# Linear attention and a gated feed-forward layer on one core: how the two weight matrices are brought in, with the column sums of w_out on TensorE and its centring on GpSimd

## The chip, the cores and the metric

The kernel runs on one core of a Trainium2 chip, as one launch. The core has five instruction queues that run beside each other: TensorE (PE in the profile, with its weight loads PEld), VectorE (DVE), ScalarE (ACT), GpSimd (POOL) and SyncE (SP, here only a queue that issues DMAs). The metric is the device time of one execution in microseconds (us), as the median of several runs; less is better. Three runs of the kernel before gave 724.57, 724.15 and 721.62 us, median 724.15 us.

## The reference

q, k and v are 8 x 8 heads of 576 x 64. Each goes through a feature map with 256 features, then linear attention; the 4608 x 512 result is the input of a feed-forward layer with a softmax gate and a layer norm.

```python
def phi(x):
    proj = np.einsum('bhsd,df->bhsf', x, w_phi)
    proj = proj - np.max(np.abs(proj), axis=-1, keepdims=True)
    return np.concatenate([np.exp(proj), np.exp(-proj)], axis=-1)
q_p, k_p = (phi(q), phi(k))
kv = np.einsum('bhsf,bhsd->bhfd', k_p, v)
z = np.sum(k_p, axis=2)
num = np.einsum('bhsf,bhfd->bhsd', q_p, kv)
den = np.einsum('bhsf,bhf->bhs', q_p, z)[..., None] + 1e-06
...                                   # x = num / den, as 4608 x 512
h = x @ w_in                          # 512 x 1024
e = np.exp(h - np.max(h, axis=-1, keepdims=True))
solu = h * e / (np.sum(e, axis=-1, keepdims=True) + 1e-09)
ln = (solu - solu.mean(-1)) / np.sqrt(solu.var(-1) + 1e-06) * g_ln
out = ln @ w_out                      # 1024 x 512
```

(The last three lines are shortened.) The weights w_in and w_out arrive as 64-bit floats.

## The kernel before, in words

The attention is done in 16 units (8 batches, 2 groups of four heads), and each unit in tiles of 128 positions. Per unit TensorE projects k and q (`pjk`, `pjq`), VectorE takes the largest absolute value (`m`) and subtracts it (`dk`, `dq`), TensorE transposes the q part (`dT`), ScalarE takes the exponentials (`ek`, `fq`), TensorE sums keys with values (`kvT`), and multiplies with the q features (`num`, `den`); GpSimd divides (`xa`, `xb`). From the fourth unit on q is projected in another form (`hq`, `pq`, `blk`, `pT`).

The feed-forward part takes 36 tiles of 128 tokens. Each needs 24 matmuls of 128x512 into `h` (high and low halves of x and of w_in: `mxh`, `mxl`, `win_h`, `win_l`) and 24 into `o` (`uhs`, `uls` with `w_out_h`, `w_out_l`). Its first tile can start only when the first batch is divided and all of `win_h` and `win_l` are there, and its first `o` when all of `w_out_h` and `w_out_l` are.

Bringing the weights in is the part that the change touches. There are eight tiles of 1 MB each, 0 to 3 of w_in and 4 to 7 of w_out. Each tile goes through these steps, whose names stand in the list of operations (line 457 on):

- `wl` (`w_load`, line 364): a DMA of the 64-bit words into `wraw`, on SP's queue.
- `ws` (`w_rebias`): ScalarE rescales the upper words, 128x1024.
- `wb` 0, 1 and 2 (`w_bits`, line 386): VectorE puts a 32-bit float `w` together from the two words, with one TENSOR_SCALAR and two SCALAR_TENSOR_TENSOR of 128x1024.
- for w_in: `wh` (ScalarE, `win_h`) and `wlo` (GpSimd, `win_l`).
- for w_out: `wg` (`w_gain`): ScalarE multiplies the rows with the layer norm's gain, 2 x 128x512. Then the mean over all 1024 rows is taken off, which stands for the layer norm's own mean: `wa` (`w_sum`) adds the four tiles on GpSimd, `cm` (`w_mean`) sums that over the partitions with two matmuls against a matrix of 1/1024, `cms` copies the result out of PSUM, `wc` (`w_center`) subtracts it on VectorE, eight times 128x512, and `woh` (ScalarE) and `wol` (GpSimd) make the high and low halves.

The order is written out: `SEQUENCE` (line 50) is a list of operation numbers, and each engine's queue holds its operations in the order in which they stand there. An engine never goes past an operation that waits. The planner's costs in the list of operations set nothing at this stage; buffers are given out in the order of `SEQUENCE` too, first in, first out for each tag. The raw tiles of w_in lie in the buffers `xa` and `xb`, where the divided attention output goes later, so tiles 0 to 3 pass through two buffers; those of w_out lie in the place of the finished `w_out_h` and `w_out_l`. Line 264 is the helper that records every instruction, so nearly all rows of the profile show that line and are told apart by their tiles.

Of the kernel before, what the change touches and what calls it, by code (L numbers as in the profile page):

```python
# [210 lines left out]
def dma(nbytes, spread=False):  # L211
    return (580 if spread else 440), max(nbytes / 300.0, 50)
# [63 lines left out]
def linear_attention_then_moe(ctx: ExitStack, tc, qT, qT2, kT, v, w_phi, w_in, g_ln, w_out, out):  # L276
# [134 lines left out]
    def w_sum(i):  # L411
        a = W[4].bitcast(F32) if i == 5 else W["sum"]
        if i == 5:
            W["sum"] = sb("e", [P, DF], F32, "wsum")
# [855 lines left out]
```

## Time and profile before

| | |
|---|---|
| median of three runs | 724.15 us |
| the profiled execution | 722.87 us |
| its span, first to last instruction | 721.1 us |
| busy: PE, PEld, DVE, ACT, POOL | 698.2, 519.0, 486.8, 369.7, 514.4 us |
| mean granted TensorE clock | 0.993 of full |
| DMA | 109.96 MB, mean 152 GB/s |

The profiled execution is 1.77 us longer than its span and 1.28 us under the median. Times in the trace count from the start of the span. A busy PE is not a PE at its peak, since matmuls are pipelined and their records overlap: the spacing of starts is the better price of one. An idle time is put down to the last event that released it.

### The profile page before, as it was taken

What the parts mean: (1) busy time and instruction counts of PE and PEld (TensorE: products, weight loads), DVE (VectorE), ACT (ScalarE), POOL (GpSimd) and SP (SyncE); (2) the same over time, 40 slices, a digit from 0 to 9 for tenths busy, and PEclk for the clock granted to TensorE, in tenths of its full rate; (3) what the DMA queues carried; (4) which work ended last, traced back from release to release, by engine and by line L of the source; (5) the groups of instructions that cost most, each with busy time, mean ns of one, the idle gap of its engine ahead of it and who ended that gap; (6) DMA issues with size and microseconds to landing.
All of it is one profiled execution on the core that took longest, in us unless ns stands there. A gap on an engine that the chain in (4) does not pass through costs nothing.

```text
span 721.1 us, 13381 instructions
## 1 busy us (share of the span) xinstructions
PE 698.2 (97%) x4858; PEld 519.0 (72%) x4858; DVE 486.8 (68%) x795; ACT 369.7 (51%) x683; POOL 514.4 (71%) x501
## 2 busy tenths in 40 slices
PE   5989799999999999999999999999999999999997
PEld 4655577777777777777767777777777777788886
DVE  5999977855777766677576668657666765446341
ACT  3878556544554564655555546436455355424131
POOL 1127799997799868888798988987777967344332
PEclk9999999999999999999999999999999999999999
DMA  7781257743654746564656365454665532521431
GB/s 265 271 263 63 68 166 207 200 141 105 192 174 126 195 148 208 141 184 135 168 160 196 122 180 163 124 155 132 180 163 141 175 107 80 170 67 53 132 128 55
DMA packets 113649, 109.96 MB, mean 152 GB/s; under 512 B 57648, under 2 KB 90928, under 8 KB 113072
## 3 DMA queue, kind: packets, MB, share of 16 engines
q1 hardware_dynamic: 113584, 109.11, 50.8%
q8 instruction: 39, 0.64, 0.4%
q14 instruction: 26, 0.21, 0.1%
HBM read 76.68 MB, written 32.39 MB: 151 GB/s over the span
## 4 chain that ended last, share of the span: by engine, by line
PE 78%; POOL 5%; DVE 2%; ACT 1%; DMA 1%; issue 1%; SPq 0%; POOLq 0%; ACTq 0%
PE o L264 25%; PE h L264 24%; PE kvT L264 9%; PE num L264 7%; PE pjk L264 4%; PE den L264 3%; PE pq L264 3%; POOL zt L264 1%; POOL hq L264 1%; POOL w_out_l L264 1%; DMA uTs<-du 1%; POOL uls L264 1%; POOL zacc L264 1%; POOL blk L264 1%; DMA rawq<-in_q 1%
## 5 line engine op out<-in xcount | busy, mean ns | idle before, releaser
L264 ACT ACTIVATE ek<-dk 128x512 f32<-128x512 f32 (+1 forms) x160 | 88.0, 583 | 65.6 <-DVE dk L264 65.1
L264 POOL TENSOR_TENSOR uls<-uTs,uhs 128x1024 fp32r<-128x1024 f32 x33 | 79.1, 2397 | 42.7 <-ACT uhs L264 34.6
L264 PE MATMUL o<-w_out_h,uhs 128*128 128x512 f32 x264 | 106.8, 405 | 0.0
L264 PE MATMUL o<-w_out_h,uls 128*128 128x512 f32 x264 | 104.2, 395 | 0.0
L264 PE MATMUL o<-w_out_l,uhs 128*128 128x512 f32 x264 | 104.1, 394 | 0.0
L264 PE MATMUL h<-win_h,mxh 128*128 128x512 f32 x288 | 93.4, 405 | 0.0
L264 PE MATMUL h<-win_l,mxh 128*128 128x512 f32 x288 | 89.6, 392 | 0.0
L264 PE MATMUL h<-win_h,mxl 128*128 128x512 f32 x288 | 89.4, 391 | 0.0
L264 POOL TENSOR_TENSOR zt<-ek 128x512 f32<-128x512 f32 x52 | 67.4, 1295 | 20.8 <-ACT ek L264 19.0
L264 DVE TENSOR_REDUCE nm<-h 128x1 f32<-128x1024 f32 x36 | 43.8, 1216 | 56.9 <-PE h L264 56.8
L264 POOL TENSOR_TENSOR hq<-rawq,hq 64x1152 fp32r<-64x1152 f32 x26 | 68.9, 2650 | 7.3 <-issue 3.4
L264 PE MATMUL num<-fq,kvf 128*64 128x288 f32 x512 | 68.9, 412 | 1.6 <-DVE eu L264 0.9
L264 ACT ACTIVATE fq<-pT 128x576 f32<-128x576 f32 x104 | 67.6, 676 | 4.8 <-DVE pT L264 4.8
L264 DVE TENSOR_REDUCE m<-pjk 128x4 f32<-128x512 f32 (+1 forms) x80 | 48.8, 623 | 31.6 <-PE pjk L264 31.4
L264 ACT ACTIVATE eu<-h,nm 128x1024 f32<-128x1024 f32 x36 | 40.2, 1118 | 55.5 <-DVE nm L264 49.7
L264 DVE STREAM_TRANSPOSE blk<-pq 128x288 f32<-128x288 f32 x104 | 45.5, 459 | 30.4 <-PE pq L264 28.1
L264 PE MATMUL kvT<-ek,rawv 128*64 128x256 f32 x512 | 63.0, 389 | 0.0
L264 PEld LDWEIGHTS h<-win_h,mxl 128*128 128x128 f32 x288 | 54.0, 188 | 12.3
L264 PEld LDWEIGHTS h<-win_l,mxh 128*128 128x128 f32 x288 | 54.0, 188 | 12.2
L264 PEld LDWEIGHTS h<-win_h,mxh 128*128 128x128 f32 x288 | 50.8, 188 | 10.5 <-issue 1.1
L264 POOL TENSOR_TENSOR blk<-blk,mcol 128x1152 f32<-128x1152 f32 x26 | 55.4, 2132 | 3.8 <-ACT mcol L264 3.0
L264 PEld LDWEIGHTS o<-w_out_h,uls 128*128 128x128 f32 x264 | 49.7, 188 | 11.7
(107 smaller groups left out, 1425.3 us busy)
## 6 DMA issues: line engine op xcount, KB each, us to landing
du<-ub SPq DMA_DIRECT2D x33, 512.0 KB, 2.8
uTs<-du SPq DMA_DIRECT2D x132, 128.0 KB, 3.1
rawq<-in_q SPq DMA_DIRECT2D x26, 576.0 KB, 5.3
rb<-d SPq DMA_DIRECT2D x64, 144.0 KB, 3.5
out<-os SPq DMA_DIRECT2D x36, 256.0 KB, 3.1
rawk<-in_k SPq DMA_DIRECT2D x32, 256.0 KB, 3.8
rawv<-in_v SPq DMA_DIRECT2D x32, 256.0 KB, 4.0
dk<-kvs SPq DMA_DIRECT2D x28, 192.0 KB, 2.0
```

The costliest lines, as they stand in the source:

```text
L264: return self.tc.keep_in_program_order(method(*args, **kwargs))
```

## The change

Four things are changed.

- All eight weight loads (`wl`) are issued from ScalarE's queue instead of SP's.
- The three GpSimd additions `wa` and the tile `wsum` are gone. `cm` now reads the four tiles themselves: eight matmuls of 128x512 instead of two, accumulating into the same bank.
- The eight subtractions `wc` run on GpSimd instead of VectorE.
- `SEQUENCE` is written anew for the shorter list of operations, so all five queues are in a somewhat different order. The operations that are not named above are the same in number and form.

```diff
 SEQUENCE = (
-    99, 88, 0, 3, 2, 126, 89, 230, 4, 102, 7, 90, 132, 103, 136, 104, 105, 127, 107, 95, 198, 91, 100, 96, 101,
...
     def w_load(i, tag):
         if i < 4:
             raw = sb(tag, [P, DF, 2], U32, f"wraw{i}")
             src = w_in[i * P : (i + 1) * P, :].bitcast(U32).rearrange("p (f two) -> p f two", two=2)
-            nc.sync.dma_start(out=raw, in_=src)
+            nc.scalar.dma_start(out=raw, in_=src)
...
-            nc.sync.dma_start(out=raw4, in_=src)
+            nc.scalar.dma_start(out=raw4, in_=src)
...
-    def w_sum(i):
-        a = W[4].bitcast(F32) if i == 5 else W["sum"]
-        if i == 5:
-            W["sum"] = sb("e", [P, DF], F32, "wsum")
-        nc.gpsimd.tensor_tensor(out=W["sum"], in0=a, in1=W[i].bitcast(F32), op=ALU.add)
-
     def w_mean():
-        cm = bank("mo", [P, DM], "cmean")
-        for c in range(2):
-            nc.tensor.matmul(
-                cm, lhsT=ones_mean, rhs=W["sum"][:, c * DM : (c + 1) * DM], start=(c == 0), stop=(c == 1)
-            )
-        W["cm"] = cm
+        cm = W["cm"] = bank("mo", [P, DM], "cmean")
+        for i in range(4, 8):
+            for c in range(2):
+                w = W[i].bitcast(F32)[:, c * DM : (c + 1) * DM]
+                nc.tensor.matmul(cm, lhsT=ones_mean, rhs=w, start=i + c == 4, stop=i + c == 8)
...
     def w_center(f):
         w = W[4 + f // 2].bitcast(F32)[:, (f % 2) * DM : (f % 2 + 1) * DM]
-        nc.vector.tensor_tensor(out=w, in0=w, in1=W["cms"], op=ALU.subtract)
+        nc.gpsimd.tensor_tensor(out=w, in0=w, in1=W["cms"], op=ALU.subtract)
...
-        op(("wl", i), "sync", dma(8 * P * DF), z - 9, w_load, (i, raw_tag[i] if i < 4 else None), alloc=[(raw_tag[i], R)] if i < 4 else [])
+        op(("wl", i), "scalar", 200, z - 9, w_load, (i, raw_tag[i] if i < 4 else None), alloc=[(raw_tag[i], R)] if i < 4 else [])
...
-    op("cm", "tensor", 2 * 855, w_mean_at, w_mean, (), [("wa", 7)], [("mo", "cm")], ["wsum"])
+    op("cm", "tensor", 8 * 430, w_mean_at, w_mean, (), [("wg", i) for i in range(4, 8)], [("mo", "cm")],
+       [("w32", i) for i in range(4, 8)])
...
-        op(("wc", f), "vector", 602, z, w_center, (f,), ["cms"], tiles=["cms", T])
+        op(("wc", f), "gpsimd", 1290, z, w_center, (f,), ["cms"], tiles=["cms", T])
```

How the new order stands is seen at three places. In the names, `wraw_107`, `wraw_109`, `wraw_113`, `wraw_115`, `wraw_146` are the raw tiles 7, 1, 0, 4 and 6 of the changed kernel.

The first is the start of ScalarE's queue. Before, the queue begins with the conversion of w_phi and with the first exponentials, and its first `ws` (tile 0) is its sixth instruction:

```order
L264 ACT_TABLE_LOAD
L264 CAST w_hh<-wph 64x128 x2
L264 ACTIVATE ek<-dk 128x2x128
L264 ACTIVATE ek<-dk 128x4x128
L264 ACTIVATE wraw_116<-wraw_116 128x1024
L264 ACTIVATE ek<-dk 128x4x128 x2
```

With the change it begins with four loads of 1 MB, and two `ws` (tiles 1 and 7) follow each other ahead of three of the first unit's exponentials:

```order
L263 DMA wraw_107<-in_w_out 128x2x1024
L263 DMA wraw_109<-in_w_in 128x2048
L263 DMA wraw_113<-in_w_in 128x2048
L263 DMA wraw_115<-in_w_out 128x2x1024
L263 ACT_TABLE_LOAD
L263 ACTIVATE ek<-dk 128x2x128 x2
L263 DMA wraw_146<-in_w_out 128x2x1024
L263 ACTIVATE ek<-dk 128x4x128
L263 ACTIVATE wraw_109<-wraw_109 128x1024
L263 ACTIVATE wraw_107<-wraw_107 128x1024
L263 ACTIVATE ek<-dk 128x4x128 x2
```

So the loads are ahead of everything else of ScalarE, and SP's queue, from which they are gone, begins with w_phi and the first k, q and v.

The second is GpSimd's queue from its first division (`xa`) to the first `mxl`, on which the first matmul of the feed-forward part waits. Before (`wsum` is the sum of the w_out tiles, `w32_4` to `w32_7` are these tiles):

```order
L264 TENSOR_TENSOR xa_639<-E_350,rb_537 128x576
L264 TENSOR_TENSOR wsum_673<-w32_4_356,w32_5_477 128x1024
L264 TENSOR_TENSOR wsum_673<-wsum_673,w32_6_643 128x1024
L264 TENSOR_TENSOR wsum_673<-wsum_673,w32_7_671 128x1024
L264 TENSOR_TENSOR hq_770<-rawq_591,hq_770 64x1152
L264 TENSOR_TENSOR win_l_99<-w32_3_563,win_h_98 128x1024
L264 TENSOR_TENSOR w_out_l_908<-w32_5_477,w_out_h_903 128x512
...
L264 TENSOR_TENSOR mxl_1138<-xa_639,mxh_1105 128x512
```

With the change (`cms_815` is the mean):

```order
L263 TENSOR_TENSOR xa_620<-E_358,rb_505 128x576
L263 TENSOR_TENSOR win_l_99<-w32_1_223,win_h_98 128x1024
L263 TENSOR_TENSOR win_l_99<-w32_3_559,win_h_98 128x1024
L263 TENSOR_TENSOR hq_659<-rawq_541,hq_659 64x1152
L263 TENSOR_TENSOR w32_4_499<-w32_4_499,cms_815 128x512
L263 TENSOR_TENSOR w32_7_281<-w32_7_281,cms_815 128x512 x2
L263 TENSOR_TENSOR xa_620<-E_653,rb_804 128x576
L263 TENSOR_TENSOR w32_5_488<-w32_5_488,cms_815 128x512
L263 TENSOR_TENSOR w_out_l_923<-w32_7_281,w_out_h_872 128x512
L263 TENSOR_TENSOR w32_6_465<-w32_6_465,cms_815 128x512 x2
...
L263 TENSOR_TENSOR mxl_1163<-xa_620,mxh_1112 128x512
```

From the mean on, the queue now holds eight subtractions, the last `win_l`, three divisions and two `w_out_l` ahead of the first `mxl`; two of the `win_l` have moved ahead of the mean. After the first `mxl` six `w_out_l` are left, against five before.

The third is TensorE around the mean. Before, `cmean` stands behind the projection `pjk` of the third unit:

```order
L264 MATMUL kvT<-ek,ones_half 32x128 x4
L264 MATMUL pjk<-wph,rawk 128x256
L264 MATMUL cmean<-wsum,ones_mean 128x512 x2
L264 MATMUL dT<-ident,dq 128x128 x6
L264 MATMUL kvt<-ident,kvs 128x128 x3
```

With the change that projection is behind it:

```order
L263 MATMUL kvT<-ek,ones_half 32x128 x4
L263 MATMUL dT<-ident,dq 128x128 x3
L263 MATMUL cmean<-w_4_499,ones_mean 128x512 x2
L263 MATMUL cmean<-w_5_488,ones_mean 128x512 x2
L263 MATMUL cmean<-w_6_465,ones_mean 128x512 x2
L263 MATMUL cmean<-w_7_281,ones_mean 128x512 x2
L263 MATMUL pjk<-wph,rawk 128x256
```

Behind the mean TensorE does the same operations as before up to the first `h`, with one `pq` pair and one group of three `dT` more, which stood behind the first `h`.

More of the change, by code (lines that the diff above doesn't have):

```diff
@@ L467, in linear_attention_then_moe @@
             op(("wg", i), "scalar", 1260, z, w_gain, (i,), [("wb", i, 2), "gain"], tiles=[T])
-    for i in range(5, 8):
-        op(("wa", i), "gpsimd", 2330, w_mean_at - 2, w_sum, (i,),
-           [("wg", 4), ("wg", 5)] if i == 5 else [("wg", i), ("wa", i - 1)], [("e", "wsum")] if i == 5 else (),
-           [("w32", 4), ("w32", 5), "wsum"] if i == 5 else [("w32", i), "wsum"])
-    op("cm", "tensor", 2 * 855, w_mean_at, w_mean, (), [("wa", 7)], [("mo", "cm")], ["wsum"])
+    op("cm", "tensor", 8 * 430, w_mean_at, w_mean, (), [("wg", i) for i in range(4, 8)], [("mo", "cm")],
+       [("w32", i) for i in range(4, 8)])
     op("cms", "scalar", 478, w_mean_at, w_mean_out, (), ["cm"], [("m2k", "cms")], ["cm"])
```

272 rows, old and new, of the table SEQUENCE are left out of this document.

## The prediction

> **What bounds the kernel now.** I read the stages first (busy time of each engine in stretches of the span; the number behind an engine is its busy time in that stretch, the last three are the granted clock, the DMA share and GB/s).
>
> ```profile
> 0.00:18.00 18.00, 10.48 (x85) 8.54 (x87) 10.45 (x19) 6.93 (x14) 2.27 (x17) 0.91 0.79 265
> ...
> 36.00:54.00 18.00, 14.87 (x186) 9.62 (x182) 18.00 (x20) 13.83 (x28) 5.14 (x2) 1.00 0.83 263
> 54.00:72.00 18.00, 16.91 (x187) 10.46 (x188) 17.05 (x26) 15.71 (x33) 13.84 (x7) 0.91 0.20 63
> 72.00:90.00 18.00, 14.04 (x148) 9.22 (x149) 16.64 (x23) 9.97 (x23) 13.13 (x7) 0.91 0.28 68
> 90.00:108.00 18.00, 17.54 (x99) 13.46 (x99) 14.31 (x24) 9.87 (x22) 17.32 (x14) 1.00 0.59 165
> 180.00:252.00 72.00, 72.00 (x517) 53.17 (x516) 54.02 (x95) 37.57 (x69) 62.39 (x54) 1.00 0.58 171
> ```
>
> And from the page, TensorE's busy tenths in 40 slices of 18 us:
>
> ```profile
> PE   5989799999999999999999999999999999999997
> ```
>
> The columns of the stages are PE, PEld, DVE, ACT, POOL. There are two regimes. From 36 to 90 us VectorE is full or nearly so (18.00, 17.05, 16.64 of 18) and TensorE has holes. From 90 us on TensorE is full, 72.00 of 72 in the row from 180, and the page has 9 in every slice up to the last. All the changed work lies in the first regime, so the time changes by as much as TensorE comes earlier, or later, to the first matmul of the feed-forward part; what follows is the same TensorE work. That matmul, and the mean's, stand here in TensorE's timeline (start, duration, and in brackets the idle time before and its releaser):
>
> ```profile
> 55.09 0.55 PE L264 MATMUL dT<-ident,dq 128*128 128x128 f32 x3 [2.27 <-ACT dn L264]
> 55.56 2.89 PE L264 MATMUL kvT<-ek,rawv 128*64 128x256 f32 x16
> 60.73 0.70 PE L264 MATMUL pjk<-wph,rawk 128*128 128x256 f32 x2
> 61.27 1.88 PE L264 MATMUL cmean<-wsum,ones_mean 128*128 128x512 f32 x4
> 62.98 0.82 PE L264 MATMUL dT<-ident,dq 128*128 128x128 f32 x6
> 65.15 1.95 PE L264 MATMUL kvT<-ek,rawv 128*64 128x256 f32 x16
> 79.00 0.55 PE L264 MATMUL dT<-ident,dq 128*128 128x128 f32 x3 [3.71 <-DVE blk L264]
> 79.47 2.91 PE L264 MATMUL kvT<-ek,rawv 128*64 128x256 f32 x16
> 86.03 2.16 PE L264 MATMUL num<-fq,kvf 128*64 128x288 f32 x16 [0.25 <-DVE blk L264]
> 89.53 0.38 PE L264 MATMUL pq<-hq,w_hh 128*128 128x288 f32 x1
> 89.88 0.63 PE L264 MATMUL h<-win_h,mxh 128*128 128x512 f32 x2
> ```
>
> The same 16 `kvT` take 1.95 us at 65.15, but 2.89 and 2.91 us behind the holes at 55.09 and 79.00, in the two stretches whose granted clock is 0.91. So a hole costs its own length, and then its neighbours run slower: 0.95 us on these 16, and with the shorter records that end the group I take 1.7 us behind each hole, an estimate.
>
> **What slows VectorE.** The view of the tile `wraw` (shortest, median, longest ns), the subtractions' row of the costliest groups to 95 us (busy us, mean ns), and the worst rows of its timeline:
>
> ```profile
> L264 DVE SCALAR_TENSOR_TENSOR w<-wraw,w x16: 1209/1218/2945, 15.6 to 73.4; 128x1024 uint32<-128x1024 uint32 x16
> L264 DVE TENSOR_SCALAR w<-wraw x8: 642/688/2865, 14.2 to 67.2; 128x1024 uint32<-128x1024 uint32 x8
> L264 DVE TENSOR_TENSOR w<-w,cms 128x512 f32<-128x512 f32 x8 | 6.8, 892 | 0.1
> 30.46 2.94 DVE L264 SCALAR_TENSOR_TENSOR w<-wraw,w 128x1024 uint32<-128x1024 uint32 x1
> 47.60 1.84 DVE L264 SCALAR_TENSOR_TENSOR w<-wraw,w 128x1024 uint32<-128x1024 uint32 x1
> 49.37 2.87 DVE L264 TENSOR_SCALAR w<-wraw 128x1024 uint32<-128x1024 uint32 x1
> 67.24 2.14 DVE L264 TENSOR_SCALAR w<-wraw 128x1024 uint32<-128x1024 uint32 x1
> 70.62 2.37 DVE L264 SCALAR_TENSOR_TENSOR w<-wraw,w 128x1024 uint32<-128x1024 uint32 x1
> 73.41 2.88 DVE L264 SCALAR_TENSOR_TENSOR w<-wraw,w 128x1024 uint32<-128x1024 uint32 x1
> ```
>
> Each long one lies beside a GpSimd instruction:
>
> ```profile
> 29.93 2.39 POOL L264 TENSOR_TENSOR win_l<-w,win_h 128x1024 fp32r<-128x1024 f32 x1 [26.89 <-ACT win_h L264]
> 48.33 3.36 POOL L264 TENSOR_TENSOR wsum<-w,w 128x1024 f32<-128x1024 f32 x1
> 54.87 5.56 POOL L264 TENSOR_TENSOR wsum<-wsum,w 128x1024 f32<-128x1024 f32 x2 [3.19 <-ACT w L264]
> 71.88 3.34 POOL L264 TENSOR_TENSOR win_l<-w,win_h 128x1024 fp32r<-128x1024 f32 x1
> 78.67 1.27 POOL L264 TENSOR_TENSOR w_out_l<-w,w_out_h 128x512 fp32r<-128x512 f32 x1 [1.24 <-ACT w_out_h L264]
> 81.06 2.35 POOL L264 TENSOR_TENSOR win_l<-w,win_h 128x1024 fp32r<-128x1024 f32 x1 [1.13 <-ACT win_h L264]
> 83.37 1.42 POOL L264 TENSOR_TENSOR xa<-E,rb 128x576 f32<-128x576 f32 x1
> 87.75 1.29 POOL L264 TENSOR_TENSOR mxl<-xa,mxh 128x512 fp32r<-128x512 f32 x1 [0.73 <-ACT mxh L264]
> ```
>
> Ahead of the mean (seven tiles) the excess over the medians is 1.72 + 0.62 + 2.18 = 4.5 us; in tile 2, behind the mean, 1.45 + 1.15 + 1.66 = 4.3 us.
>
> **The parts, with their costs.** All times are on the trace of 722.87 us.
>
> *Loads on ScalarE's queue.* Issuing costs ScalarE about 0.45 us a load:
>
> ```profile
> L264 SPq DMA_DIRECT2D wraw<-in_w_in x4: 340/431/576, 4.4 to 47.6; - x4
> 11.58 1.13 ACT L264 ACTIVATE wraw<-wraw 128x1024 f32<-128x1024 f32 x1 [0.80 <-DMA wraw<-in_w_in]
> 14.00:16.00 2.00, 2.00 (x26) 1.95 (x24) 1.93 (x4) 0.58 (x2) 0.00 (x0) 0.64 0.98 365
> ```
>
> Four of the eight go out while ScalarE still waits for w_phi, so the issuing itself is hidden. But 4.2 MB now compete with the first k, q and v, and the transfers run at 365 GB/s where they are full. The first two `ws` want 2.1 MB: at half of 365 GB/s that is 11.5 us, from about 2 us on, so 13.5 us, against 11.58 before. VectorE reaches its first weight step at 14.2 us (first row of `TENSOR_SCALAR` above), with the `ws` of 1.13 us in between. Bounds: 0, and 10 us if the loads are served ahead of all else (4.2 MB / 365 GB/s = 11.5 us, less what SP can issue). I take 1.0 us late, since half each is nearest to what two full queues would do.
>
> The Trainium skill, *DMA: Bandwidth & Descriptors*, section "Issuing engines are not separate DMA queues", says that another issuing engine adds no DMA engine and saves issue time alone, and its section on queues that the engines take turns between the queues. By turns the start is late by the 1.0 us taken; no run here has two queues.
>
> *The three additions gone, eight matmuls for two.* Two matmuls of the mean start at 61.27, and the next begins at 62.98: 1.71 us, 0.855 each. Eight take 6.84 us, 5.13 us more TensorE work, in a stage where TensorE has holes. The mean needs no GpSimd any more, so it starts when TensorE gets there and the last gain (`wg`) is done:
>
> ```profile
> 55.80 1.33 ACT L264 ACTIVATE w<-w,gcol 128x512 f32<-128x512 f32 x2 [0.47 <-DVE w L264]
> 63.18 0.59 ACT L264 COPY cms<-cmean 128x512 f32<-128x512 f32 x1 [0.20 <-PE cmean L264]
> ```
>
> The gain ends at 57.13; 4.5 earlier and 1.0 later, at 53.6. TensorE: 61.27, less `pjk` that now stands behind (0.54), less 4.5, plus 1.0, is 57.2 with the slow clock from 55.56 on and 55.5 without it. I take 56.0. The mean then ends at 62.8, against 62.98: up to here the change wins nothing.
>
> *From the mean to the first `h`.* Before, that took 89.88 - 62.98 = 26.9 us, of which 3.96 are holes that wait for VectorE (3.71 + 0.25) and 1.7 slow clock. VectorE loses the eight subtractions from this stretch (6.8 us by eight times their mean of 0.89) and can be ahead by that much, so I take these 5.7 us as gone; I add `pjk` (0.54) and the `pq` pair and `dT` that moved ahead (0.35 and 0.47 by the starts of the rows behind them, 0.8 together). That is 22.6 us, so the first `h` starts at 85.4. Since 0.8 us of work that stood behind it now lies before it, TensorE is 89.88 + 0.8 - 85.4 = 5.3 us ahead.
>
> *Centring on GpSimd.* From the mean to the first `mxl` its queue holds eight subtractions at 1.27 (the `w_out_l` row, the same two-input form), three divisions at 1.42, one `win_l` at 2.35, two `w_out_l` at 1.27, and the `mxl` of 1.29: 10.2 + 4.3 + 2.35 + 2.5 + 1.3 = 20.6 us. From `cms` at 63.4 that ends at 84.0: hidden by 1.4 us, if nothing blocks it. ScalarE holds its `woh` in order behind each subtraction, with the exponentials for TensorE behind them. I take 1.0 us for such new waits, between 0 and the 4.3 us of tile 2's excess.
>
> **Sum:** +1.0 (start), -4.5 (bits), +5.13 (mean) and the rest as above: 5.3 - 1.0 = 4.3 us less, 718.6 us against the profiled 722.87. On the median, 1.28 us above that execution, 719.9 us.
>
> **Rivals.**
>
> *GpSimd takes VectorE's place (0.24).* If the subtractions and the bits of tile 2 block each other as at 71.88 and 73.41, the first `mxl` comes at 84.0 + 4.3 = 88.3, `h` at 88.6, and the gain is 2.0 us; one more `w_out_l` (1.27) is left for the stretch from 90 us, where GpSimd is at 17.32 of 18, so 0.7 remains: 723.4 us. For it: GpSimd gets 10.2 us of work and loses 8.9. Against it: it idles 3.19, 1.24 and 1.13 us in the rows above. The Trainium skill, *SBUF — State Buffer*, section "Who interferes with whom", has it that a VectorE instruction with two SBUF inputs and a GpSimd instruction that reads SBUF exclude each other for a whole instruction; the row of 2945 ns agrees, and by that rule the centring is this rival's case wherever it meets tile 2.
>
> *The order does not keep them apart (0.12).* Nothing but the queues does so. Then the 4.5 us stay: mean at 60.5, its end at 67.3, `h` at 89.9, gain 0.75: 723.4 us.
>
> *The start is late (0.14).* If the four loads hold up the first k and q by 10 us instead of 1, VectorE starts later by as much and nothing returns it: 719.9 + 9 = 729 us. It costs the whole gain from a delay of 5.2 us on, and makes the kernel slower by 0.5% from 8.8 us on. Against it: small loads and large ones lie on different queues, and SP's first now are w_phi and k.
>
> **Numbers.** 0.5% is 3.6 us, about what this kernel's three runs (721.62 to 724.57) can tell from nothing. The forecast has 0.50, and 719.9 lies just beyond that bound; its own range is 715.5 (mean at 54, no new waits: `h` at 83.4, 7.3 us ahead, and a faster run) to 721. With the two rivals at 723.4 and part of the third the range reaches to 726. Faster 0.50, same 0.36, slower 0.14.
>
> **What would show it.** Right: no weight step over 1.4 us ahead of the mean; `cmean` with 16 records over 6.8 us from about 56; no hole of over 1 us between it and the first `h`; that `h` at 84 to 87 us. Wrong: the first `pjk` or the first `ws` late by over 3 us; GpSimd full from the mean to the first `mxl` with TensorE waiting; a new hole after 90 us, since I take what follows as unchanged work; or a TensorE waiting for the mean long enough to run its eight matmuls at a low clock.

## The result, and the profile after

The changed kernel takes 733.99 us (median of four runs, 733.68 to 734.9) beside 723.43 us for the kernel before (median of four, 721.62 to 724.57): a ratio of 1.0151, interval 1.0135 to 1.0167. It is slower by 1.5%, where 719.9 us and a gain were forecast, and it lies outside the range of 715.5 to 726. The profiled execution took 733.68 us, its span is 731.8 us (721.1 before). Of the kernels below, one execution of the one with mean and centring in the old order took 3711.0 us and was a slow one, so it is left out of the ratio, and the median of its ten does not feel it.

TensorE's timeline of the changed kernel, the rows that answer to those of the prediction (start, duration, and in brackets the idle time before and its releaser):

```profile
12.80 3.20 PE L263 MATMUL pjk<-wph,rawk 128*128 128x256 f32 x18 [12.80 <-DMA rawk<-in_k]
19.36 2.75 PE L263 MATMUL pjq<-wph,rawq 128*128 128x256 f32 x18 [2.21 <-issue]
67.78 7.13 PE L263 MATMUL cmean<-w,ones_mean 128*128 128x512 f32 x16 [1.99 <-DVE dq L263]
74.75 0.59 PE L263 MATMUL pjk<-wph,rawk 128*128 128x256 f32 x2
100.50 0.71 PE L263 MATMUL h<-win_h,mxh 128*128 128x512 f32 x2
```

Of the same view of the kernel before, the first row:

```profile
4.98 3.20 PE L264 MATMUL pjk<-wph,rawk 128*128 128x256 f32 x18 [4.98 <-DMA wph<-in_w_phi]
```

TensorE starts 7.82 us later, and the first `h` comes at 100.50 instead of 89.88, 10.62 us later. The span is 10.7 us longer, so next to nothing more is lost behind the first `h`. The stages of the changed kernel say the same (columns PE, PEld, DVE, ACT, POOL, then granted clock, DMA share, GB/s):

```profile
0.00:18.00 18.00, 4.35 (x34) 3.54 (x34) 3.07 (x7) 2.03 (x4) 2.25 (x17) 1.00 0.89 327
18.00:36.00 18.00, 14.56 (x152) 10.84 (x154) 15.06 (x25) 13.77 (x27) 0.00 (x0) 0.91 0.57 194
72.00:90.00 18.00, 17.14 (x177) 11.07 (x177) 11.39 (x17) 11.90 (x27) 14.18 (x10) 1.00 0.30 82
180.00:252.00 72.00, 72.00 (x480) 54.05 (x478) 50.73 (x87) 39.35 (x73) 59.84 (x52) 1.00 0.57 160
```

In the first 18 us TensorE worked 4.35 us instead of 10.48, and VectorE 3.07 instead of 10.45, while the DMA engines were busier than before (0.89 against 0.79). From 180 us on TensorE is full, as before. What filled the DMA engines stands in the queues' view for 0 to 14 us (packets, MB, share of 16 engines), first of the changed kernel, then of the kernel before:

```profile
q10 hardware_dynamic: 664, 3.57, 64.6%
q1 hardware_dynamic: 816, 0.95, 20.9%
```

```profile
q1 hardware_dynamic: 1767, 3.30, 73.2%
```

And the same view for what was issued by 2.2 us, with its size and the median time to landing, first of the changed kernel, then of the kernel before:

```profile
wraw<-in_w_out ACTq DMA_DIRECT2D x1, 1024.0 KB, 5.3
wph<-in_w_phi SPq DMA_DIRECT2D x1, 32.0 KB, 6.7
rawk<-in_k SPq DMA_DIRECT2D x1, 256.0 KB, 9.3
```

```profile
rawk<-in_k SPq DMA_DIRECT2D x1, 256.0 KB, 3.0
```

q10 is ScalarE's queue with the weights. It moved 3.57 MB while SP's queue, with all of w_phi, k, q and v, moved 0.95 MB. The first large k was under way from 1.8 to 11.1 us, so SP's queue had work all that time; over these 9.3 us the same view gives the weights 3.15 MB in 551 packets and SP's queue 0.33 MB in 288. The first weight tile (issued at 0.72) landed at 6.0 us, the first half of w_phi (issued at 1.14) at 7.8, the first large k (issued at 1.78) at 11.1. The same k landed 3.0 us after its issue before.

Two further rows show ScalarE and SP held up in the issuing itself:

```profile
11.07 0.39 ACTq L263 DMA_DIRECT2D wraw<-in_w_out  x1
11.49 1.28 ACT L263 ACT_TABLE_LOAD   x1 [11.49 <-DMA rawk<-in_k]
```

```profile
5.99 6.78 SPq L263 DMA_DIRECT2D rawq<-in_q  x3
```

The listing of the changed program names what they wait for:

```text
4 L263 DMA wraw_115<-in_w_out 128x2x1024 [waits DMAHW2_49]
6 L263 DMA rawq_111<-in_q 128x512 [waits DMAHW0_49]
7 L263 DMA rawq_117<-in_q 128x512 [waits DMAHW1_49]
8 L263 DMA rawq_119<-in_q 128x128 [waits DMAHW3_49]
```

The program has eight semaphores for the completion of transfers and deals them out in turn, over all queues. A ninth transfer is not issued before an earlier holder of its semaphore has landed. So the fourth weight load, on ScalarE's queue, waited until k had landed (11.1 us), with ScalarE's work behind it; and the first q went out at 5.99, when the first weight tile, issued at 0.72 with 5.3 us to landing, was there (SP's waits have 1.6 us for it). A 1 MB tile early in the list thus holds back small loads on another queue too. ScalarE lost nothing by its own wait here, since its first exponential waits for VectorE's `dk` until 14.95. This is read from the listing and from two times that agree; no run took the semaphores alone away.

The second place is ahead of the mean. VectorE's last four SCALAR_TENSOR_TENSOR steps there, and GpSimd beside them, of the changed kernel:

```profile
57.67 8.66 DVE L263 SCALAR_TENSOR_TENSOR w<-wraw,w 128x1024 uint32<-128x1024 uint32 x4
55.90 1.42 POOL L263 TENSOR_TENSOR xa<-E,rb 128x576 f32<-128x576 f32 x1 [14.67 <-DMA rb<-d]
57.28 2.37 POOL L263 TENSOR_TENSOR win_l<-w,win_h 128x1024 fp32r<-128x1024 f32 x1
62.60 2.63 POOL L263 TENSOR_TENSOR win_l<-w,win_h 128x1024 fp32r<-128x1024 f32 x1 [2.95 <-ACT win_h L263]
75.67 3.75 POOL L263 TENSOR_TENSOR w<-w,cms 128x512 f32<-128x512 f32 x3 [6.87 <-ACT cms L263]
98.38 1.30 POOL L263 TENSOR_TENSOR mxl<-xa,mxh 128x512 fp32r<-128x512 f32 x1
```

At 1218 ns each (the median of before) the four would take 4.9 us; they took 8.66, 3.8 us more, in the order that was to keep them apart. GpSimd's division waited for `rb`, the broadcast of the divisors, which in SP's new order stands behind loads that wait for buffers (`d` is stored at 40.65, the first `rb` is issued at 45.62, the second at 48.51, and it takes 7.2 us to land among those loads); so `win_l`, behind that division in GpSimd's queue, came into the bits. (The last two rows are the first subtractions and the first `mxl`, for later.)

### The profile page after: what moved, and what is told of

Its sections match the earlier page's. It is cut to its first block, busy times and chain, and to the rows that moved or that the text cites. A ratio compares the mean times of both kernels' runs of the same rounds, so it can differ in the third digit from the quotient of the medians.

```text
span 731.8 us, 13357 instructions
## 1 busy us (share of the span) xinstructions
PE 702.9 (96%) x4870; PEld 518.9 (71%) x4870; DVE 479.9 (66%) x787; ACT 371.3 (51%) x683; POOL 515.8 (70%) x506
## 4 chain that ended last, share of the span: by engine, by line
PE 74%; DVE 8%; DMA 7%; POOL 4%; ACT 3%; SPq 2%; issue 2%; POOLq 0%; ACTq 0%; DVEq 0%
PE h L263 24%; PE o L263 24%; PE kvT L263 7%; PE num L263 7%; PE pjk L263 4%; PE pq L263 3%; PE den L263 3%; DVE w L263 2%; SPq L263 2%; DMA rawq<-in_q 1%; DMA wph<-in_w_phi 1%; DVE m L263 1%; DMA rawv<-in_v 1%; DMA rawk<-in_k 1%; DVE dk L263 1%
## 5 line engine op out<-in xcount | busy, mean ns | idle before, releaser
L263 DVE STREAM_TRANSPOSE pT<-blk 128x288 f32<-128x288 f32 x104 | 42.0, 446 | 40.8 <-POOL blk L263 38.9
L263 PE MATMUL pjk<-wph,rawk 64*128 64x128 f32 (+1 forms) x544 | 48.9, 297 | 15.0 <-DMA rawk<-in_k 14.1
L263 PE MATMUL kvT<-ek,rawv 128*64 128x256 f32 x512 | 61.0, 380 | 0.0
L263 PEld LDWEIGHTS pjk<-wph,rawk 64*128 64x128 f32 (+1 forms) x544 | 37.7, 192 | 30.5 <-issue 22.5
```

The lines of the kernel that those rows point to most:

```text
L263: return self.tc.keep_in_program_order(method(*args, **kwargs))
```

## The experiments

The kernels below take the change apart by place, by part and by cost. Ratios are to runs of the kernel before on the same chip, in brackets the interval.

### Where the first loads stand

**The four first loads issued later**, the rest as changed:

```diff
 ScalarE, operations of the list
-wl 7, wl 1, wl 0, wl 4   (at the front)
 ek (first)
+wl 1, wl 7
 ek, ek
+wl 0, wl 4
```

> The changed kernel with its four first weight loads issued later: two behind the first exponential on ScalarE's queue, two behind the next two; all else as changed. Theory (the loads in ScalarE's queue hold up the first w_phi, k and q): the first pjk starts at 5 to 6 us instead of 12.80, and the 7.8 us by which it was late come back, less up to 2 us because k's and q's later loads now meet the weights: first h at 93 to 95 us, 726 to 728 us. Rival (the start has slack, the loss is made by the meetings of bits and GpSimd from 57 us on): the first pjk comes early but the first h stays at 99 to 101, 732 to 734 us.

Measured: 738.0 us, 1.019 (1.0155 to 1.0225), slower than either expected, with the first `h` at 106.28 in the profiled execution (741.19 us, the longest of the four). The first `pjk` was early, but the wait had moved to q and to ScalarE:

```profile
5.75 3.20 PE L263 MATMUL pjk<-wph,rawk 128*128 128x256 f32 x18 [5.75 <-DMA rawk<-in_k]
22.14 2.08 PE L263 MATMUL pjq<-wph,rawq 64*128 64x128 f32 x16 [9.16 <-DMA rawq<-in_q]
24.08 1.14 ACT L263 ACTIVATE wraw<-wraw 128x1024 f32<-128x1024 f32 x1 [12.53 <-DMA vz<-in_v]
```

ScalarE stood still for 12.5 us: two issues of weight tiles stand ahead of its first `ws`, and its queue is in order. That q was issued only at 14.15, and took 7.9 us to land. Before the issue, SP's queue had waited for the first of the moved weight tiles, with which it shares a semaphore by the listing (SP's waits from 7 to 16 us: us in total, times, longest):

```profile
SPq L263 <- DMA wraw<-in_w_in: 5.6, 1, 5.6
```

So weight tiles ahead of q cost no less than ahead of k, and of the 9.16 us that TensorE waits up to 5.6 are the semaphore's rather than the shared transfer's (an estimate from these two rows).

**The kernel before with three loads at the front**, on ScalarE's queue:

```diff
-            nc.sync.dma_start(out=raw, in_=src)
+            nc.scalar.dma_start(out=raw, in_=src)
 # and in the list
+wl 4, wl 0, wl 1 at the very front
```

> The kernel before with only the loads changed: all eight on ScalarE's queue and three of them (4, 0, 1) at its very front; additions, mean and centring as before. Theory: the first pjk starts at 10 to 13 us instead of 4.98 and the whole program is late by as much: 729 to 732 us, the cost of the change without the rest of it. Rival (the delay is absorbed by slack at the start): 723 to 725 us.

Measured: 727.23 us, 1.0054 (1.0035 to 1.0074), with the first `pjk` as late as the theory said:

```profile
10.01 3.20 PE L264 MATMUL pjk<-wph,rawk 128*128 128x256 f32 x18 [10.01 <-DMA wph<-in_w_phi]
```

Of 5.0 us at the start 4.4 are left in the profiled spans (725.5 against 721.1), 3.8 in the medians (727.23 against 723.46): most of a late start stays, but less than all of it. The time lies between the two ranges, under the theory's 729 to 732.

**The kernel before with the queue alone** (the same edit of `w_load`, the list as it was):

> The kernel before with all eight weight loads on ScalarE's queue, each at its old place in the written order (behind the same operations). What the queue alone does. Theory (it is the place at the front that costs, not the queue): first pjk at 5 us, 722 to 725 us. Rival (a second queue with large rows takes the transfer engines from k and q wherever it stands): the first pjk or the first tiles behind it are late by 3 us or more, 726 us or more.

Measured: 724.7 us, 1.0015 (1.0001 to 1.0029), first `pjk` at 4.70, as the theory had it. The queue costs about 1 us (0.1 to 2.1 by the interval); the place at the front costs the other 2.5 of the 3.8 us.

**Loads with short rows** (the edit in short):

```diff
-            nc.scalar.dma_start(out=raw, in_=src)
+            for b in range(2):
+                nc.scalar.dma_start(out=out[:, :, b], in_=src[:, :, b])   # rows of 1 KB, w_out in four
```

> The changed kernel with each weight load cut into pieces whose rows are 1 KB instead of 4 or 8 KB (two issues for a tile of w_in, four for one of w_out), same bytes, same queue, same place. Theory A (the transfer engines take turns between the two queues by packets, so the bytes go by the length of the packets): with equal packets the k and w_phi loads get half instead of a fifth, the first pjk comes at 7 to 10 us instead of 12.80, and 728 to 732 us. Theory B (first come, first served: SP's loads wait for the bytes that were issued before them): the first pjk stays at 12 to 14 us, 733 to 736 us.

Measured: 735.13 us, 1.0157 (1.0129 to 1.0184). The `pjk` is where theory A had it, the time where theory B had it:

```profile
8.58 3.20 PE L263 MATMUL pjk<-wph,rawk 128*128 128x256 f32 x18 [8.58 <-DMA rawk<-in_k]
14.63 2.15 PE L263 MATMUL pjq<-wph,rawq 64*128 64x128 f32 x16 [2.85 <-DMA rawq<-in_q]
17.50 1.28 ACT L263 ACT_TABLE_LOAD   x1 [17.50 <-DMA wraw<-in_w_out]
```

It doesn't tell the theories apart: cutting also made issuing slower (twelve issues ahead of ScalarE's first work, 17.50 instead of 11.49), so fewer bytes stood ahead of k when it was issued, which would bring it earlier under B as well. How the engines choose between two queues stays open. The delay went on to q and to ScalarE.

**The loads back on SP's queue**, at their new places in the list:

```diff
-            nc.scalar.dma_start(out=raw, in_=src)
+            nc.sync.dma_start(out=raw, in_=src)
```

> The changed kernel with the weight loads back on SP's queue, at their places in the new written order (two behind w_phi, the first k and a v; two more behind the first q); all else as changed. Theory (a second queue with long rows takes the transfer engines from k): the first pjk starts at 4 to 6 us instead of 12.80, 7.8 us come back less up to 3 us for q's loads, which still stand behind 2 to 4 MB: 726 to 729 us. Rival (it is the place in the order and not the queue: every transfer waits for the completion semaphore of the one eight places ahead, so 1 MB tiles early in the order hold up all that follows on any queue): the first pjk is early, but TensorE has holes of 5 us or more before q, and 731 to 735 us.

Measured: 737.93 us, 1.0203 (1.0171 to 1.0235). The rival's sign, k early and q late, and beyond its range:

```profile
5.66 3.20 PE L263 MATMUL pjk<-wph,rawk 128*128 128x256 f32 x18 [5.66 <-DMA rawk<-in_k]
12.31 2.15 PE L263 MATMUL pjq<-wph,rawq 64*128 64x128 f32 x16 [3.45 <-DMA rawq<-in_q]
18.38 1.19 PE L263 MATMUL pjq<-wph,rawq 128*128 128x256 f32 x2 [3.92 <-DMA rawq<-in_q]
23.37 2.08 PE L263 MATMUL pjq<-wph,rawq 64*128 64x128 f32 x16 [3.79 <-DMA rawq<-in_q]
```

k is early, and q late three times over, 11.2 us in all, though no wait has the 5 us that the rival named. Whichever queue they go by, the tiles ahead have to be moved first. Up to 30 us SP's queue waits 6.9 us for weight tiles to land before it can issue, so the semaphores have a part in it; the run does not tell it from that of the bytes.

**The old start**: the first 137 operations (some 36 us) in the order of before, the rest new; loads on SP's queue.

> The changed kernel with the first 137 operations of the list (up to the first store of a divisor, some 36 us) in the old order, loads on SP's queue; mean, centring and all that follows in the new order. Theory (the loss is made at the start, 8 us or more, and about 3 us more by the late rb): first pjk at 5 us, no wait for q over 2.5 us, first h at 91 to 94, 725 to 728 us. Rival (the new order behind 36 us is itself worse, the start only part of it): first h at 96 or later, 730 us or more.

Measured: 726.97 us, 1.0051 (1.0029 to 1.0073), first `h` at 92.95, as the theory had it (one wait for q is 2.67 us, just over its 2.5):

```profile
92.95 0.70 PE L263 MATMUL h<-win_h,mxh 128*128 128x512 f32 x2
```

Against its pair with the new start (737.93) that is 11 us from the order of the first 36 us alone. Against the changed kernel itself (733.99), whose loads lie on ScalarE's queue, it is 7.0 us, near the 7.8 us by which that one starts late.

**The old start, 100 operations only** (with the early rb of the next part):

> As before with only the first 100 operations in the old order (some 28 us; five of the eight loads lie there), rb early. Theory (only the places of the first loads matter, and they are all among the first 100): within 1.5 us of the run with 137 and early rb. Rival (the new order between 28 and 36 us costs too): 2 us or more slower than it.

Measured: 729.48 us, 1.0078 (1.0057 to 1.0098), 4.4 us slower than with 137 (725.12, below): the rival. Only one weight load lies between 100 and 137 in the old order, so the loads don't explain it; the joint of the two orders makes a hole:

```profile
34.92 1.54 PE L263 MATMUL dT<-ident,dq 128*128 128x128 f32 x6 [6.39 <-ACT fq L263]
```

The run says that the two orders join badly at 100, and nothing of what either is worth between 28 and 36 us.

### The late broadcasts

**rb right behind the store of d**, once with the new start on SP's queue, once with the old start:

```diff
 SP, operations of the list
 ds 0
+db 0 0, db 0 1
 vl, kl, vl (wait for buffers)
-db 0 0
 ...
-db 0 1
```

> As the run with the loads back on SP's queue, and the broadcasts of the first divisors (rb) moved right behind the store of d, ahead of the k, q and v loads that wait for buffers. Theory (the late rb pushes GpSimd's division and win_l into the bits at 57 to 66 us): the four STT ahead of the mean take about 4.9 us together instead of 8.66, and the run is 2 to 4 us faster than its pair without the move. Rival (TensorE has other work there, the lost VectorE time is slack): within 1 us of its pair.

> As the run with the old start, and the first two broadcasts of a divisor (rb) right behind its store. Theory (late rb costs 3 us, as the pair on SP's queue gave): 722 to 725 us, the bits ahead of the mean at their undisturbed 1.2 us each. Rival (rb comes in time anyway, since SP's loads there wait less with the old start): within 1 us of its pair.

Measured: 734.92 us, 1.016 (1.013 to 1.019), 3.0 us less than its pair; and 725.12 us, 1.0014 (0.9996 to 1.0032), 1.85 us less than its pair. In both pairs the intervals overlap a little; in the first, all four times lie below all four of the pair. The first pair shows the mechanism; of the run with early rb:

```profile
60.96 4.63 DVE L263 SCALAR_TENSOR_TENSOR w<-wraw,w 128x1024 uint32<-128x1024 uint32 x4
58.36 2.39 POOL L263 TENSOR_TENSOR win_l<-w,win_h 128x1024 fp32r<-128x1024 f32 x1
64.77 3.06 POOL L263 TENSOR_TENSOR win_l<-w,win_h 128x1024 fp32r<-128x1024 f32 x1 [4.02 <-ACT win_h L263]
```

GpSimd is done at 60.75, the four steps begin at 60.96 and take 4.63 us. In the pair this `win_l` ran until 61.52 and the steps, from 60.83 on, took 7.38: the division that stands ahead of it came only 0.8 us later there (57.75 against 56.99). Of the 2.75 us that VectorE gains, 1.6 are there at the first `h` (100.81 against 102.37); the rest of the 3.0 us in the time lies behind it and is not put down to the bits.

The second pair shows the same steps, without and with early rb:

```profile
49.53 8.01 DVE L263 SCALAR_TENSOR_TENSOR w<-wraw,w 128x1024 uint32<-128x1024 uint32 x4
50.92 4.62 DVE L263 SCALAR_TENSOR_TENSOR w<-wraw,w 128x1024 uint32<-128x1024 uint32 x4
```

The mean starts 1.82 us earlier with it (58.49 against 60.31). At the first `h` 0.2 us of that are left in the profiled execution, and its span is 0.3 us longer (724.7 against 724.4), so the 1.85 us in the time rest on the medians.

### Mean and centring

**The mean alone** (the change's `w_mean`, without `wa`), in the old order:

> The kernel before with the mean taken by eight matmuls and the three GpSimd additions gone; loads, centring and order as before. Prediction's terms: 4.5 us less of stretched bits ahead of the mean (3.7 of it in the two that met an addition), 5.13 us more TensorE work: first h within 1 us of 89.88, 722 to 725 us. Rival (the holes at 55.09 and 79.00 close as VectorE gets ahead): 719 to 721 us. Rival (the eight matmuls stand fully on the path): 727 to 729 us.

Measured: 724.71 us, 1.0019 (1.0003 to 1.0035); first `h` at 92.85. The time is in the range, the `h` is 3 us late instead of within 1 (and the two steps that met an addition make 0.62 + 2.18 = 2.8 us of the 4.5, not 3.7): the mean runs at 59.15, 2.1 us earlier than before, and ends 3.0 us later (66.02 against 62.98).

**Mean and centring** in the old order:

> The kernel before with the mean by eight matmuls and the centring on GpSimd; loads and order as before. All of the change but the loads and the new order. Prediction's sum without the start: 718 to 721 us. Rival (the centring meets the bits of tile 2, which stand in the old order right behind the mean, and GpSimd becomes the wait for the first mxl): 723 to 727 us.

Measured: 726.73 us, 1.0039 (1.0024 to 1.0053): the rival. GpSimd is full from 72 to 90 us (18.00 in the fifth column), and TensorE still has its hole, with another releaser:

```profile
72.00:90.00 18.00, 13.63 (x148) 9.37 (x146) 13.48 (x19) 10.87 (x24) 18.00 (x11) 0.91 0.28 68
79.70 0.90 PE L263 MATMUL dT<-ident,dq 128*128 128x128 f32 x3 [3.65 <-ACT E L263]
79.25 0.40 ACT L263 COPY E<-num 128x288 f32<-128x288 f32 x1 [3.50 <-POOL xa L263]
```

Before, that hole was 3.71 us behind VectorE's `blk`. Now TensorE waits for ScalarE's `E`, and that for GpSimd's division `xa`, which stands behind four subtractions, a `win_l` and a `w_out_l` in GpSimd's queue.

**205 operations in the old order**, so that only the mean and what follows are new:

> As before with the first 205 operations in the old order (some 48 us, nearly all bits ahead of the mean), rb early; only the mean, the centring and what follows are in the new order. Theory (the new order from the mean on is what was worth something: it closes the 3.71 us hole ahead of the first h): 719 to 723 us. Rival (the mean's 5.1 us stand on the path and eat that): 724 to 727 us, as with mean and centring in the old order.

Measured: 727.25 us, 1.0049 (1.0027 to 1.0071), just above the rival's range. The joint has a fault of its own here too: the last three bit steps ahead of the mean take 7.88 us, beside two `win_l`.

**A cheap mean** tells what the eight matmuls cost. It reads the upper 16 bits of each weight alone:

```diff
-    ones_mean = const.tile([P, P], F32, name="ones_mean")
+    ones_mean = const.tile([P, P], BF16, name="ones_mean")
...
-                w = W[i].bitcast(F32)[:, c * DM : (c + 1) * DM]
+                w = W[i].bitcast(BF16).rearrange("p (f two) -> p f two", two=2)[:, c * DM : (c + 1) * DM, 1]
```

> The run with the old start of 137 operations and early rb, with a mean that reads only the upper 16 bits of each weight (bf16), so the mean is taken of cut weights; else the same. Theory (the mean's eight f32 matmuls stand on the path): they take under 2 us instead of 6.9 and 4 to 5 us come back: 720 to 721.5 us. Rival (from the mean on GpSimd and its centring are the path): the time comes back as a wait of TensorE ahead of the first h, 723.5 to 725.5 us.

> The run with the mean only (old order, centring on VectorE), with the mean of the upper 16 bits. Theory: 724.7 less 4 to 5 us, 719.5 to 721 us, under before, since the additions and their meetings with the bits are gone and the mean costs no more than its old two matmuls. Rival (VectorE, full to 90 us, is what TensorE waits for: holes at dT and blk grow by what the mean gives back): 723 to 725 us.

> The run with mean and centring in the old order, with the mean of the upper 16 bits. Theory (matmuls on the path): 726.7 less 4 to 5 us, 721.5 to 723 us. Rival (GpSimd, 18.00 of 18 from 72 to 90 us, is the path to the first mxl): it starts earlier by as much as the mean ends earlier, up to 5 us, so the rival gives the same unless TensorE waits for mxl by over 1 us: then 724 us or more.

Measured, each against its pair with the full mean: 722.36 us, 0.9981 (0.9969 to 0.9993), 2.8 us less; 721.21 us, 0.9962 (0.9948 to 0.9975), 3.5 us less; 720.1 us, 0.9955 (0.9939 to 0.9972), 6.6 us less. In the last of them (mean and centring in the old order):

```profile
57.74 1.97 PE L264 MATMUL cmean<-w,ones_mean 128*128 128x512 bf16 x8
59.55 0.82 PE L264 MATMUL dT<-ident,dq 128*128 128x128 f32 x6
73.35 0.90 PE L264 MATMUL dT<-ident,dq 128*128 128x128 f32 x3 [3.61 <-ACT E L264]
87.37 0.62 PE L264 MATMUL h<-win_h,mxh 128*128 128x512 f32 x2
```

The eight take 1.81 us, 0.23 each, where the f32 form took 6.97. Of these 5.2 us about half and two thirds come back in the first two pairs, between theory and rival (the runs of a pair were taken on different chips; by the ratios to the kernel before it is 2.4 and 4.1 us). In the profiled executions the first `h` is 4.0 and 3.8 us earlier, so the matmuls stand on the path for the larger part. In the third it is more than all, 6.6 us. The first `h` is 6.4 us earlier there and the subtractions on GpSimd, which is full, begin 6.4 us earlier (60.47 against 66.83); but 1.3 of that are there before the mean begins (57.74 against 59.05), for which no row gives a reason, so the matmuls give back some 5.1 us, an estimate. All three beat the kernel before, by 0.2, 0.4 and 0.5%, and the last is the fastest of the kernels here. Its mean is that of weights cut to 16 bits.

**The centring back on VectorE**, with old start, early rb and cheap mean:

```diff
-        nc.gpsimd.tensor_tensor(out=w, in0=w, in1=W["cms"], op=ALU.subtract)
+        nc.vector.tensor_tensor(out=w, in0=w, in1=W["cms"], op=ALU.subtract)
```

> The run with old start, early rb and cheap mean, with the centring back on VectorE. Theory (VectorE idles behind the mean in the new order, 18 us have 12 us of work, so it can take 5 us of centring, and GpSimd, 15.7 of 18, is relieved): 1 us or more faster than with the centring on GpSimd. Rival (VectorE then delays what TensorE waits for): 1 us or more slower.

Measured: 722.5 us, 0.9976 (0.9958 to 0.9995), against 722.36 with GpSimd: no difference, neither expectation. GpSimd falls from 14.58 to 9.49 us of 18 from 72 to 90 us and the time stays. The first `h` is 1.1 us earlier in the profiled execution (87.61 against 88.74), of which the times show nothing. So in this order the place of the centring decides little.

## Why the prediction was wrong

By its own steps, on the profiled execution. The first `h` was put at 85.4 and came at 100.5, 15.1 us later. The terms that make this up: 6.8 (start) + 3.8 (bits) + 1.2 (what is left ahead of the mean, not put down to a row; as much as the prediction took off there for the slow clock, 57.2 to 56.0) + 0.1 (mean) + 3.2 (behind it) = 15.1. With the 1.0 us of new waits that the sum had already set aside, 14.1 us are left, and 719.9 + 14.1 = 734.0, the measured median. That it meets the median to the tenth is luck: from the first `h` to the end of the span the profiled executions here took 630.1 to 633.1 us.

**The step that failed is the first, "+1.0 (start)".** It measured 7.8 us, and is the largest of the misses; by itself it would have made 726.7 us of the 719.9, and the bits and the way behind the mean, below, make the rest. Two things in it were wrong. The share: "at half of 365 GB/s" was taken for the weights, and they got 3.57 MB of 4.52 in 14 us. And the question: the step asked when the first `ws` has its tiles and found that VectorE doesn't want them before 14.2 us. It never asked when k and q have theirs. The `ws` were late too (18.51 against 11.58), but it was k that TensorE waited for, and behind the first k, q. The row was there: the DMA engines were 0.79 busy in the first 18 us before, at 265 GB/s, so a transfer put ahead of k can only push k back. The Trainium skill, *DMA: Bandwidth & Descriptors*, has it in its section "Queues, rings and completion order" that each engine takes turns between the queues, a packet at a time. The prediction made equal shares of bytes of that; the trace has 3.57 against 0.95 MB, and while k was under way 3.15 against 0.33 MB, 551 against 288 packets as the profile counts them. The three transfers that were followed landed in the order of their issue (first weight tile 6.0, w_phi 7.8, k 11.1 us).

*The rival "the start is late" (0.14)* named the right mechanism, with 10 us for 7.8. Its price of 729 us was too low by 5, because it kept the whole gain of the other terms; and its counter-argument, that small and large loads lie on different queues and SP's first are w_phi and k, carried no weight: the queues share the transfer engines and the eight semaphores.

*Bits ahead of the mean, -4.5.* 3.8 us of excess were there in another place. The rival "the order does not keep them apart" (0.12) was right for this stretch. Cause: the `rb` on SP. The prediction costed the orders of GpSimd and VectorE, and not the queue that feeds GpSimd, though a moved step's DMAs and the queues it is moved past belong to its cost. With `rb` early the order does keep them apart (four steps in 4.63 and 4.62 us).

*The mean, 8 x 0.855 = 6.84 us.* Right: 67.78 to 74.75, 6.97 us. That it does not wait for GpSimd was right as well; it waited 1.99 us for VectorE's `dq` instead.

*From the mean to the first h, 22.6 us.* It took 25.75. VectorE's hole of 3.71 us is gone, as forecast, and VectorE is at 11.39 of 18 from 72 to 90 us. In its place stand three short ones that were set at 1.0 us together:

```profile
87.47 1.46 PE L263 MATMUL pjk<-wph,rawk 64*128 64x128 f32 x16 [0.86 <-ACT fq L263]
93.34 0.37 PE L263 MATMUL pq<-hq,w_hh 128*128 128x288 f32 x1 [0.88 <-DVE dk L263]
95.89 0.40 PE L263 MATMUL pq<-hq,w_hh 128*128 128x288 f32 x1 [0.43 <-ACT fq L263]
```

They make 2.2 us; the other 1.0 us is not put down to a row. That no hole exceeds 1 us here came out as the prediction said.

*Centring on GpSimd, hidden by 1.4 us.* From the first subtraction (75.67) to the end of the first `mxl` (99.68) it took 24.0 us where 20.6 were worked out, and ended 0.8 us ahead of the first `h`. Hidden, but worth nothing either: with a cheap mean the place of the centring makes 0.1 us in the medians.

*What no step said:* the gain was small to begin with. With a clean start, the bits kept apart and the centring on GpSimd the kernel is at 725.12 us (0.9996 to 1.0032), where the sum without its start term gives 718.9. The mean's +5.13 weighs what it was said to weigh, and stands on the path; the terms set against it came to less: 2.1 us of excess are left in the old start (one step of 3.34 us, as the 2.94 at 30.46 before, which lay beside a `win_l` and not beside an addition), and the way from the mean to the first `h` takes 27.4 us there. Part of the latter is a slower `num` (3.44 us for 16, 2.16 elsewhere) in that one execution.

## What to carry to other kernels

Where the DMA engines are near full at the start of a program, price a load that moves forward by what it pushes back, in bytes ahead of the first operand that TensorE needs, on whatever queue; a second queue makes no room. When an order is rewritten to keep two engines apart, check the third queue that feeds one of them: here a broadcast on SP, late by some us, undid the order. And work moved to TensorE from an engine with time to spare is on the path unless TensorE's holes shrink by as much: it wants the cheapest form of matmul first (0.23 against 0.855 us), where its result allows it.

## What the runs showed of the hardware

- Two queues did not share by halves: 3.57 and 0.95 MB in the first 14 us of the changed kernel, and 3.15 and 0.33 MB (551 and 288 packets) while k was under way. By what rule is open.
- An issue that waits for a completion semaphore held all that stood behind it in its queue: in the first experiment ScalarE did no work for 12.53 us behind two weight loads, and SP issued nothing for 5.6 us until a weight tile of ScalarE's queue had landed.
- A bf16 matmul of 128x512 that reads every second 16-bit word of SBUF took 0.23 us (mean and centring with the cheap mean), the f32 form 0.855 us (before).
- VectorE's steps with two inputs and GpSimd's `win_l` are sensitive to less than 1 us: with the division 0.8 us earlier, four steps took 4.63 us instead of 7.38.
